# Attention with packed keys, then a token-mixing MLP, on one core: all steps in a new order, with TensorE's short steps spread over its blocks of 256 instructions

## The chip, the core and the metric

The kernel runs on one core of a Trainium2 chip. The core has a matrix engine (TensorE, in the profile PE, its weight loads PEld), a vector engine (VectorE, DVE), an activation engine (ScalarE, ACT), a general engine (GpSimd, POOL) and a queue engine (SyncE, SP). Each engine works through its own instructions in the order in which they were written, and waits on semaphores for what other engines or transfers must have done. The metric is the device time of the whole program in microseconds (us). The kernel before takes 109.34 us, the median of three runs.

## The reference

Eight batches, eight heads, 576 tokens, 64 wide; 32 packed queries p for each head. All inputs and the output are float32 in memory.

```python
def sm_attn(qq, kk, vv):
    s = scale * np.matmul(qq, kk.transpose(0, 1, 3, 2))
    s = s - np.max(s, axis=-1, keepdims=True)
    a = np.exp(s)
    a = a / (np.sum(a, axis=-1, keepdims=True) + 1e-09)
    return np.matmul(a, vv)
p_packed = sm_attn(p, k, v)
out = sm_attn(q, p_packed, p_packed)          # B, H, S, 64
...
x = out.transpose(0, 2, 1, 3).reshape(B, S, 512)
wq = x @ w_q                                  # 512 -> 64
wk = x @ w_k
W_tok = scale * np.einsum('bsd,btd->bst', wq, wk)
mixed = np.einsum('bst,btd->bsd', W_tok, x)
return np.maximum(mixed, 0.0) @ w_out
```

## The kernel before

The whole kernel is a list of some 700 steps, the string `ORDER`, and a loop at the end that walks through it. An item is `NAME.batch.part@ENGINE=banks`: `X1.2.0@A` is step X1 of batch 2, part 0, on ScalarE (A; V is VectorE, P is GpSimd), and `S1.2=4,5,2,3` is a TensorE step that writes the PSUM banks 4, 5, 2 and 3. No scheduler comes behind it: on each engine the instructions stand in the order of the items. Semaphores between engines are placed by the framework from what a step reads and writes, PSUM banks included: a step that writes a bank waits until the last reader of it is done.

For each batch b the steps are:

- Loads, all issued by GpSimd's queue: `LD.k`, `LD.v` (two transfers), `LD.q`; batch 0 has k in two halves `LD.g0` and `LD.h0` and q in two halves `LD.r0` and `LD.q0`, batch 7 `LD.r7` and `LD.q7`. `LD.P0` to `LD.P3` bring the packed queries, `LD.W0` and `LD.W1` w_k and w_q, `LD.O` w_out (tile `wout`). Each of k, v and q has four buffers (NL = 4). The loads turn float32 into bfloat16.
- `KT` (VectorE, line 244) turns k round in blocks of 32x32; `S1` (TensorE, lines 277 and 287) makes the scores of the packed queries; `X1` (ScalarE) their exponentials; `TE` (VectorE) turns them round. Batches 0 and 1 need no `TE`, but the block diagonal of p (`EC`, `EX`, `PB`); the others need `PX`.
- `PV` (TensorE, line 318) multiplies with v, whose buffers carry a block of ones for the sums (`SET.v`); `RC` and `PP` (VectorE) divide and mask, `PT` turns round. The result is p_packed.
- `QK` (TensorE, line 339) is p_packed times w_k and w_q, `QKE` copies it out of PSUM and `QD` (GpSimd) doubles a part of it.
- `QV` (VectorE) turns q round; `S2` (TensorE, line 376) makes the scores of the second attention, in parts 0, 1, 2 (batches 0, 1, 7) or 3 and 2; `X2` (ScalarE) their exponentials; `RS`, `RR` (VectorE) sums and reciprocals (for batch 5 `HA` on GpSimd halves the sum first); `AM` (VectorE or GpSimd, line 408) multiplies: the weights a.
- `AT` (TensorE, lines 417 and 422) turns a round, `AE` copies it out of PSUM; `WKQ` (TensorE, lines 444 and 449) makes wk and wq from it, `WE` copies; `GM` (line 470), `GE`, `Y` (line 480), `YE`, `MX` (line 495), `MR` (line 501) make the mixed tokens; `RL`, `RLR` and `RLF` (ScalarE or VectorE) the maximum with 0.
- `OT` (TensorE, line 543, four matmuls of 128x512 each; `OH` half as wide) multiplies with w_out; `OE`, `OEF` and `OEH` copy to SBUF; `ST`, `STF` and `STH` store, on SP's queue. SP first runs `HOLD.v7`, which waits for the last load of v, so that no store runs beside the loads before it.

`WARM.n=bank` (line 614) is n matmuls of 128x512 whose result nobody reads. They stand where TensorE would have nothing to do, the first 27 ahead of the first step S1.0. One block of TensorE's program in what follows is 256 instructions; each matmul is two, a weight load and the multiplication.

Eight PSUM banks are shared by all steps; `T["s1", b]`, `T["mx", b, i]` and the like hold which banks a later step reads. The step loop:

```python
else:
    bk = [int(z) for z in bk.split(",")] if bk else None
    steps[f[0]](*[int(z) for z in f[1:]], eng,
                bk[0] if bk and len(bk) == 1 else bk)
```

## Time and profile before

| | before |
|---|---|
| median of 3 runs | 109.34 us (109.15 to 109.53) |
| the profiled execution | 109.69 us |
| its span, first to last instruction | 107.6 us |
| granted TensorE clock | 1.0 throughout |
| busy: TensorE, VectorE, ScalarE, GpSimd | 96.4, 78.2, 66.3, 49.1 us |
| loads through GpSimd's queue | 15.08 MB |
| stores through SP's queue | 9.50 MB |

The profile is one execution. A line of the chain of waits has the start, the length and what ran or was waited for; `issue` is time in which the engine waited for nothing that the profile shows. A line of the timeline has start, length, engine, source line, operation, tiles and shapes, and in brackets the idle time before it with what ended that. A line of the groups has the count, then total busy time and the mean in ns of one, then idle time before them. The line of a helper (244 for all 32x32 transposes, 131 and 135 for copies) stands for all steps that use it. The loads keep the DMA engines busy from about 3 us to about 78 us, at some 210 GB/s.

### The profile page before, as it was taken

The numbers are of one execution on the slowest core, as the hardware profiler recorded it, in microseconds if no ns is written. First come the engines' busy times: TensorE is split into PE (matmuls) and PEld (weight loads), VectorE is DVE, ScalarE is ACT, GpSimd is POOL, SyncE is SP. The second block draws the span as 40 slices with busy tenths as digits, with TensorE's granted clock in tenths as the row PEclk, the third lists the DMA queues.
The fourth block names the chain that finished last, engine by engine and source line by source line (L and its number), as shares of the span: only waits on it lengthen the run. The fifth ranks groups of instructions, "written<-read, shape, count | busy, mean of one in ns | idle before, by whom it ended". The sixth has DMA issues, their size and how long they took to land.

```text
span 107.6 us, 3612 instructions
## 1 busy us (share of the span) xinstructions
PE 96.4 (90%) x1547; PEld 53.2 (49%) x1547; DVE 78.2 (73%) x151; ACT 66.3 (62%) x104; POOL 49.1 (46%) x75
## 2 busy tenths in 40 slices
...
GB/s 51 143 173 196 210 209 201 216 208 206 206 211 211 209 213 207 209 210 213 212 206 213 214 202 213 215 204 215 218 398 395 411 270 299 254 387 328 195 371 129
DMA packets 13935, 24.87 MB, mean 231 GB/s; under 512 B 2144, under 2 KB 7008, under 8 KB 13920
## 3 DMA queue, kind: packets, MB, share of 16 engines
q0 software_dynamic: 10016, 15.08, 78.7%
q1 hardware_dynamic: 3632, 9.50, 22.9%
q8 instruction: 12, 0.20, 0.7%
...
q14 instruction: 3, 0.02, 0.1%
...
## 4 chain that ended last, share of the span: by engine, by line
PE 60%; DMA 10%; POOL 7%; ACT 7%; DVE 6%; issue 5%; ACTq 0%; POOLq 0%; DVEq 0%
PE ps L543 26%; DMA wqk<-in_moe_w_q_dram 10%; PE ps L376 4%; PE ps L318 4%; PE ps L422 4%; PE ps L449 3%; PE ps L614 3%; PE ps L495 3%; PE ps L287 3%; PE ps L444 3%; DVE rs L397 2%; PE ps L470 2%; POOL a L408 2%; PE ps L339 2%; ACT aT L131 2%
## 5 line engine op out<-in xcount | busy, mean ns | idle before, releaser
L543 PE MATMUL ps<-wout,relu 128*128 128x512 bf16 x124 | 30.9, 380 | 0.5 <-ACT e1T L298 0.5
L408 POOL TENSOR_TENSOR a<-e,rr 128x256 bf16<-128x256 f32 (+2 forms) x15 | 15.9, 1070 | 23.3 <-ACT e L381 6.5
L614 PE MATMUL ps<-o 128*128 128x512 bf16 x79 | 21.1, 406 | 1.9 <-DVE o L138 1.9
L381 ACT ACTIVATE e<-ps 128x256 f32<-128x256 f32 (+2 forms) x19 | 11.2, 622 | 13.2 <-PE ps L376 13.0
L131 ACT ACTIVATE o<-ps 128x1024 f32<-128x1024 f32 (+2 forms) x18 | 15.8, 882 | 2.2 <-PE ps L543 2.1
L543 PEld LDWEIGHTS <-relu 128*128 128x128 bf16 x124 | 10.7, 98 | 11.7 <-issue 2.0
L244 DVE STREAM_TRANSPOSE kT<-k_sb 128x1152 uint32<-128x1152 uint32 (+1 forms) x9 | 11.2, 1243 | 3.2 <-DMA k_sb<-in_k_dram 3.2
L506 ACT ACTIVATE relu<-ps 128x1024 bf16<-128x1024 f32 (+1 forms) x11 | 13.0, 1218 | 0.6 <-PE ps L501 0.6
L397 DVE TENSOR_REDUCE rs<-e 128x16 f32<-128x512 f32 (+2 forms) x13 | 11.1, 856 | 2.4 <-ACT e L381 2.4
L614 PEld LDWEIGHTS <-o 128*128 128x128 bf16 x79 | 7.4, 104 | 10.4 <-issue 2.4
L244 DVE STREAM_TRANSPOSE qT<-q_sb 128x1152 uint32<-128x1152 uint32 (+1 forms) x10 | 11.0, 1107 | 0.0
L179 POOL DMA_DIRECT2D v_sb<-in_v_dram x16 | 10.2, 647 | 0.3 <-issue 0.3
L298 ACT ACTIVATE e1T<-ps 128x576 bf16<-128x576 f32 x12 | 7.3, 650 | 2.7 <-PE ps L287 2.6
L244 DVE STREAM_TRANSPOSE e<-e1T 128x576 bf16<-128x576 bf16 x12 | 8.7, 746 | 0.2
L295 ACT ACTIVATE e<-ps 128x1152 bf16<-128x1152 f32 x2 | 2.3, 1132 | 9.6 <-PE ps L277 9.6
L508 DVE TENSOR_SCALAR relu<-ps 128x1024 bf16<-128x1024 f32 (+1 forms) x7 | 7.7, 1131 | 0.1
L318 PE MATMUL ps<-v_sb,e 64*64 64x192 bf16 x288 | 7.7, 245 | 0.0
L376 PE MATMUL ps<-ppT,qT 64*128 64x64 bf16 x320 | 6.6, 190 | 1.3 <-issue 1.1
L376 PEld LDWEIGHTS <-qT 64*128 64x128 bf16 x320 | 5.7, 94 | 4.1 <-issue 2.1
L318 PEld LDWEIGHTS <-e 64*64 64x64 bf16 x288 | 5.8, 106 | 2.1 <-issue 1.4
L131 ACT ACTIVATE wkq<-ps 128x896 bf16<-128x896 f32 (+1 forms) x8 | 6.2, 778 | 1.0 <-PE ps L449 0.8
L449 PE MATMUL ps<-aT,pqk 128*128 128x256 bf16 (+1 forms) x48 | 6.7, 246 | 0.0
...
## 6 DMA issues: line engine op xcount, KB each, us to landing
out_dram<-o SPq DMA_DIRECT2D x14, 512.0 KB, 4.9
...
```

Of the source, the lines that this page charges most:

```text
L131: nc.scalar.activation(o, i, COPY)
L179: nc.gpsimd.dma_start(v_bufs[b % NL][halves(i), 0:7:2], src)
L244: nc.vector.transpose(o, i)
L318: nc.tensor.matmul(T["pv", b][halves(cc), i], lhsT, rhs, start=n == 0, stop=n == R - 1, skip_group_check=True)
L376: nc.tensor.matmul(ps[:, y, t - t0, i], lhsT, rhs, start=e == 0, stop=e == 1)
L381: nc.scalar.activation(e2[:, t0:t1].rearrange("a t (i y n) -> a y (t i) n", i=2, y=2), T["s2", b, c].rearrange("a y t i n -> a y (t i) n") ...
L397: nc.vector.tensor_reduce(rs[:, t0 * H:t1 * H], src, axis=AX, op=ADD)
L408: e.tensor_tensor(a2[:, t0:t1].rearrange("a t i (u l) -> a (t i u) l", l=L), e2v(b, c), T["rr", b][:, t0 * H:t1 * H].to_broadcast((P, (t1 ...
L449: nc.tensor.matmul(o, pqk[:, i, Dl:], aT[:, i, c0:c1], start=i == 0, stop=i == 1)
L506: nc.scalar.activation(o, i, RELU)
L543: nc.tensor.matmul(ps, lhsT, wout[:, j, :], start=j == 0, stop=j == NJ - 1)
L614: nc.tensor.matmul(ps, warm[:, 0:P], warm, start=True, stop=True)
```

## The change

Nothing but `ORDER` changes: the same steps in another sequence, some of them on another engine or in other banks.

```diff
--- before.py
+++ after.py
@@ -10,53 +10,53 @@
 TURN = tuple(range(8))
 
 ORDER = """
-LD.E1@A LD.E0@S LD.g0 LD.h0 SET.v2@P LD.r0 LD.W0 SET.pz0@V SET.aT1@V SET.aT0@V SET.warm@V SET.idf@V
-SET.v0@V SET.tab@A EC@V EX@V SET.aff@P LD.v0 KT.0.0@V PB.0.2@V SET.mask@V KT.0.1@V PB.0.3@V QV.0.0@V
-LD.q0 PB.0.1@A LD.k1 PB.0.0@P WARM.27=3 S1.0=0,1,2 X1.0.0@A WARM.12=3 PV.0.0=0,1 PV.0.1 RC.0@V LD.W1
-SET.v1@P LD.P0 LD.v1 PP.0.0@V PP.0.1@V QV.0.1@V PT.0@V SET.v3@P LD.q1 LD.P1 LD.P2 LD.P3 WARM.8=2
-S2.0.2=0,1 X2.0.2@A RS.0.2@V KT.1.2@V RR.0.2@V S2.0.1=4,5 S2.0.0=2,3 X2.0.1@A WARM.5=6 QK.0=0
-X2.0.0@A SET.idb@V RS.0.1@V RS.0.0@V QKE.0@V RR.0.1@V RR.0.0@V LD.k2 LD.O AM.0.1@P WARM.2=2
-S1.1=3,4,5 X1.1.0@A WARM.5=2 PV.1.0=4,5 PV.1.1 RC.1@V PP.1.0@V PP.1.1@V AM.0.0@V PT.1@V QV.1.2@V
-AT.0.1=3 WARM.5=0 AT.0.0=2 QK.1=4 QD.0@P LD.v2 AM.0.2@P LD.q2 WARM.4=5 S2.1.2=0,1 S2.1.0=6,7 PX@V
-X2.1.2@A AT.0.2=5 S2.1.1=0,1 X2.1.0@A AE.0.2@A X2.1.1@A RS.1.2@V AE.0.0@V RR.1.2@V WKQ.0.0=6,7 LD.k3
-AM.1.2@P WKQ.0.2 WARM.1=0 AT.1.2=1 AE.0.1@V RS.1.1@V QKE.1@A WKQ.0.1 RR.1.1@V AM.1.1@P LD.v3 LD.k4
-KT.2.2@V RS.1.0@V WE.0.0@A AE.1.2@A WE.0.1@A WARM.3=4 GM.0=6 GE.0@V RR.1.0@V AM.1.0@V S1.2=4,5,2,3
-AT.1.1=7 Y.0=0,1 X1.2.0@A AE.1.1@V X1.2.1@A LD.q3 QD.1@P YE.0@A WARM.3=6 AT.1.0=4 AE.1.0@A TE.2.1@V
-MX.0.1=0,1 MR.0=2,3 TE.2.0@V MX.0.0=4,5 RL.0.1@A RLR.0@A RL.0.0@A WKQ.1.0=6,7 WKQ.1.2 WKQ.1.1
-PV.2.0=0,1 PV.2.1 WE.1.0@V WE.1.1@V RC.2@V PP.2.1@V PP.2.0@V PT.2@V QV.2.2@V GM.1=6 GE.1@A WARM.1=7
-Y.1=4,5 OT.0.0=0,1 YE.1@A MR.1=4,5 MX.1.0=6,7 WARM.2=2 S2.2.3=2,3 RLR.1@A X2.2.3@A RL.1.0@V
-S2.2.2=4,5 OT.0.1 X2.2.2@A KT.3.2@V LD.v4 RS.2.4@V RR.2.4@V SET.aT2@V OE.0.0@A MX.1.1=6,7 OT.1.4=2
-S1.3=4,5,0,1 X1.3.0@A QK.2=3 OEF.1.4@A X1.3.1@A RL.1.1@A QKE.2@A TE.3.0@V AM.2.3@V TE.3.1@V
-OT.0.2=4,5 OT.0.3 LD.q4 LD.k5 AM.2.2@P LD.v5 QD.2@P AT.2.2=0 WARM.1=1 AT.2.3=6 PV.3.0=2,3 PV.3.1
-AE.2.3@A WKQ.2.0=6,7 OE.0.1@A KT.4.2@V AE.2.2@V RC.3@V WKQ.2.1 WKQ.2.2 WE.2.2@A S1.4=0,1,4,5
-PP.3.1@V PP.3.0@V PT.3@V QV.3.2@V OT.1.0=2,3 QK.3=6 GM.2=7 X1.4.1@A X1.4.0@A S2.3.2=4,5 QKE.3@A
-TE.4.1@V TE.4.0@V X2.3.2@A GE.2@A S2.3.3=0,1 X2.3.3@A Y.2=4,5 OT.1.1 YE.2@V RS.3.4@V MX.2.0=6,7
-MX.2.1=0,1 PV.4.0=4,5 PV.4.1 OE.1.0@A RR.3.4@V RC.4@V OT.1.2=2,3 PP.4.0@V PP.4.1@V LD.k6 LD.q5
-QD.3@P AM.3.3@P AM.3.2@P PT.4@V QV.4.2@V RL.2.1@A RL.2.0@A OT.1.3 MR.2=4,5 QK.4=0 RLR.2@V OE.1.1@A
-QKE.4@A AT.3.3=1 AE.3.3@V S2.4.3=6,7 S2.4.2=2,3 X2.4.2@A X2.4.3@A AT.3.2=5 WKQ.3.0=0,1 AE.3.2@V
-KT.5.2@V WKQ.3.1 WKQ.3.2 OT.2.2=2,3 WE.3.2@A RS.4.4@V S1.5=6,7,4,5 GM.3=1 OT.2.3 X1.5.0@A X1.5.1@A
-GE.3@V LD.v6 QD.4@P Y.3=6,7 OE.2.1@A OT.2.0=4,5 TE.5.0@V YE.3@V RR.4.4@V LD.q6 LD.k7 AM.4.3@P
-AM.4.2@P LD.v7 LD.r7 LD.q7 TE.5.1@V MX.3.0=6,7 MX.3.1=0,1 MR.3=2,3 RLR.3@A OT.2.1 PV.5.0=2,3
-RL.3.1@V KT.6.2@V RL.3.0@A OE.2.0@A PV.5.1 AT.4.3=6 AT.4.2=7 OT.3.0=0,1 AE.4.3@A RC.5@V PP.5.1@V
-PP.5.0@V AE.4.2@V QV.5.2@V PT.5@V S1.6=2,3,4,5 WKQ.4.0=6,7 X1.6.0@A X1.6.1@A WKQ.4.1 WKQ.4.2
-TE.6.0@V TE.6.1@V OT.3.1 WE.4.2@A S2.5.2=4,5 S2.5.3=2,3 X2.5.2@A OE.3.0@A GM.4=7 X2.5.3@A PV.6.0=4,5
-GE.4@V Y.4=6,7 PV.6.1 QK.5=0 YE.4@V RC.6@V MX.4.1=6,7 QKE.5@A MX.4.0=2,3 PP.6.0@V PP.6.1@V PT.6@V
-QV.6.2@V RL.4.1@A OT.3.2=0,1 HA.5@P RS.5.4@V RR.5.4@V AM.5.3@P OT.3.3 RL.4.0@A S2.6.2=6,7 S2.6.3=4,5
-X2.6.2@A MR.4=2,3 QK.6=7 X2.6.3@A OE.3.1@A RLR.4@V KT.7.2@V HOLD.v7 OT.3.4=6 OT.4.0=4,5 RS.6.4@V
-S1.7=0,1,2,3 QKE.6@A OEF.3.4@A X1.7.1@A X1.7.0@A QD.5@P AM.5.2@P QD.6@P AT.5.3=7 AE.5.3@V RR.6.4@V
-OT.4.1 AT.5.2=2 AE.5.2@A WKQ.5.0=0,1 AM.6.3@P AM.6.2@P WKQ.5.1 WKQ.5.2 OE.4.0@A OT.4.2=2,3 WE.5.2@A
-OT.4.3 GM.5=0 TE.7.1@V TE.7.0@V QV.7.0@V QV.7.1@V GE.5@V AT.6.3=7 AT.6.2=6 OE.4.1@A Y.5=0,1 AE.6.2@A
-YE.5@A AE.6.3@V PV.7.0=4,5 ST.0.0 ST.0.1 ST.1.4 ST.1.0 ST.1.1 ST.3.4 ST.2.0 ST.3.1 ST.4.0 PV.7.1
-MR.5=0,1 RC.7@V RLR.5@A MX.5.1=6,7 MX.5.0=2,3 RL.5.1@A PP.7.0@V PP.7.1@V WKQ.6.0=0,1 WKQ.6.1 WKQ.6.2
-PT.7@V RL.5.0@V OT.5.4=4 WE.6.2@A S2.7.0=2,3 S2.7.2=0,1 S2.7.1=6,7 X2.7.2@A RS.7.2@V GM.6=5 X2.7.0@A
-OEF.5.4@A X2.7.1@A OT.5.2=0,1 GE.6@V RS.7.0@V RR.7.2@V AM.7.2@P Y.6=2,3 QK.7=5 YE.6@V RR.7.0@V
-OT.5.3 AT.7.2=2 QKE.7@A RS.7.1@V RR.7.1@V AE.7.2@A AM.7.1@V AM.7.0@P QD.7@P MX.6.1=6,7 MX.6.0=4,5
-RL.6.0@V RL.6.1@V OE.5.1@A OT.5.0=2,3 AT.7.0=0 AT.7.1=1 AE.7.0@A OT.5.1 AE.7.1@A WKQ.7.0=4,5 WKQ.7.2
-WKQ.7.1 WE.7.0@V OT.6.0=6,7 OE.5.0@V WE.7.1@A GM.7=4 OT.6.1 GE.7@A ST.5.4 ST.3.0 ST.5.1 ST.4.1
-ST.2.1 ST.5.0 OE.6.0@A ST.6.0 Y.7=2,3 MR.6=4,5 YE.7@V RLR.6@V OT.6.2=0,1 MX.7.1=6,7 MR.7=4,5
-MX.7.0=2,3 RLR.7@V OT.6.3 RLF.7.0.1@V RLF.7.0.0@V RLF.7.1.0@A RLF.7.1.1@A OT.7.4=5 OE.6.1@A OH.7.0=2
-OT.7.2=6 ST.6.1 OEF.7.4@A OEH.7.0@A OEF.7.2@A STH.7.0 ST.7.4 STF.7.2 OT.7.1=2 OEF.7.1@A STF.7.1
-OT.7.0=5 OH.7.1=6 OEF.7.0@A OEH.7.1@A STF.7.0 STH.7.1
+LD.E0@S LD.E1@A SET.pz0@V SET.aT0@V SET.warm@V SET.tab@A EC@A EX@V SET.v1@V SET.idf@V PB.0.2@V LD.h0
+SET.v3@P LD.g0 SET.v0@P LD.v0 LD.q0 SET.mask@P PB.0.0@P PB.0.3@V KT.0.1@V KT.0.0@V PB.0.1@V
+WARM.21=1 S1.0=0,2,4 X1.0.0@A WARM.5=3 PV.0.0=0,1 PV.0.1 RC.0@V QV.0.1@V PP.0.0@V PP.0.1@V LD.r0
+LD.k1 LD.W1 LD.W0 SET.aff@P SET.idb@V PT.0@V QV.0.0@V WARM.11=2 S2.0.2=0,1 S2.0.0=2,3 LD.v1 LD.P3
+LD.q1 LD.P2 SET.v2@V KT.1.2@V LD.P1 LD.P0 S2.0.1=4,5 X2.0.1@A X2.0.0@A X2.0.2@A RS.0.1@V SET.aT1@V
+RS.0.0@V RR.0.1@V RS.0.2@V RR.0.2@V RR.0.0@V AM.0.0@V AM.0.2@V SET.aT2@V WARM.10=6 S1.1=0,1,2
+X1.1.0@A WARM.6=3 PV.1.0=0,1 PV.1.1 AT.0.0=3 AT.0.2=5 LD.k2 LD.v2 LD.q2 AM.0.1@V RC.1@V PP.1.0@V
+AE.0.2@V PP.1.1@V PT.1@V AT.0.1=2 WARM.3=4 QK.1=0 QKE.1@A QK.0=1 QKE.0@A AE.0.0@V LD.k3 QD.0@P
+QD.1@P LD.O QV.1.2@V WARM.6=3 S2.1.2=0,1 S2.1.1=4,5 S2.1.0=6,7 AE.0.1@A X2.1.1@A PX@V WARM.2=2
+WKQ.0.0=4,5 WKQ.0.2 RS.1.1@V X2.1.0@A WKQ.0.1 X2.1.2@A WE.0.0@A RS.1.0@V RR.1.1@V WE.0.1@A KT.2.2@V
+RS.1.2@V RR.1.0@V RR.1.2@V AM.1.0@V LD.v3 AM.1.1@P LD.k4 AM.1.2@V WARM.3=1 GM.0=0 WARM.3=5 AT.1.1=4
+S1.2=2,3,6,7 GE.0@A AE.1.1@A Y.0=0,1 YE.0@A AT.1.0=4 AE.1.0@V X1.2.1@A AT.1.2=0 X1.2.0@A AE.1.2@A
+WARM.1=1 MR.0=6,7 WKQ.1.0=4,5 MX.0.1=2,3 RLR.0@V TE.2.0@V TE.2.1@V WKQ.1.2 WKQ.1.1 MX.0.0=6,7
+WARM.1=0 PV.2.0=0,1 QV.2.2@V WE.1.0@A PV.2.1 WE.1.1@A RC.2@V PP.2.1@V GM.1=4 GE.1@V PP.2.0@V
+RL.0.0@A RL.0.1@A PT.2@V WARM.6=5 S2.2.2=2,3 KT.3.2@V S2.2.3=0,1 QK.2=4 Y.1=6,7 X2.2.2@A X2.2.3@A
+QKE.2@A YE.1@V RS.2.4@V WARM.3=2 MX.1.1=6,7 S1.3=0,1,2,3 X1.3.1@A X1.3.0@A RL.1.1@A OT.0.0=4,5
+OT.0.2=2,3 OT.0.3 TE.3.1@V RR.2.4@V AM.2.2@V OT.0.1 AT.2.2=0 OE.0.1@A TE.3.0@V PV.3.0=6,7 PV.3.1
+LD.q3 LD.v4 LD.q4 QD.2@P LD.k5 AM.2.3@V LD.k6 OE.0.0@A AE.2.2@A AT.2.3=2 MR.1=0,1 MX.1.0=4,5 RC.3@V
+AE.2.3@V PP.3.0@V KT.4.2@V PP.3.1@V PT.3@V RLR.1@A RL.1.0@A WARM.1=3 WKQ.2.0=0,1 WKQ.2.2 WKQ.2.1
+OT.1.4=2 WE.2.2@A LD.v5 S1.4=6,7,4,5 OEF.1.4@A GM.2=0 X1.4.1@A QV.3.2@V OT.1.0=2,3 GE.2@A X1.4.0@A
+Y.2=4,5 YE.2@A S2.3.2=6,7 S2.3.3=0,1 X2.3.2@A TE.4.0@V TE.4.1@V X2.3.3@A MX.2.1=4,5 OT.1.1
+MX.2.0=0,1 PV.4.0=6,7 PV.4.1 RS.3.4@V RL.2.1@A OE.1.0@A RL.2.0@A OT.1.2=4,5 RC.4@V RR.3.4@V PP.4.1@V
+PP.4.0@V LD.q5 AM.3.3@P OT.1.3 PT.4@V QV.4.2@V OE.1.1@A QK.4=7 MR.2=0,1 QK.3=6 AM.3.2@V AT.3.3=2
+AT.3.2=3 S2.4.2=4,5 AE.3.3@V RLR.2@A QKE.3@A AE.3.2@A QKE.4@A X2.4.2@A S2.4.3=0,1 KT.5.2@V X2.4.3@A
+QD.3@P WKQ.3.0=2,3 WKQ.3.2 WKQ.3.1 OT.2.2=4,5 WE.3.2@A RS.4.4@V S1.5=0,1,6,7 GM.3=2 X1.5.1@A OT.2.3
+KT.6.2@V GE.3@A X1.5.0@A Y.3=6,7 OT.2.0=2,3 YE.3@A OE.2.1@A MX.3.0=6,7 MX.3.1=0,1 RR.4.4@V TE.5.1@V
+TE.5.0@V RL.3.0@A OT.2.1 RL.3.1@V PV.5.0=4,5 OE.2.0@A LD.v6 LD.q6 AM.4.3@P LD.k7 LD.v7 QD.4@P
+AM.4.2@V PV.5.1 S1.6=0,1,6,7 RC.5@V AT.4.3=2 AT.4.2=3 PP.5.0@V PP.5.1@V OT.3.0=4,5 X1.6.0@A X1.6.1@A
+AE.4.3@V AE.4.2@V PT.5@V TE.6.0@V QV.5.2@V TE.6.1@V WKQ.4.0=6,7 WKQ.4.1 WKQ.4.2 OT.3.1 QK.5=2
+WE.4.2@A OE.3.0@A GM.4=3 GE.4@V MR.3=6,7 S2.5.3=0,1 Y.4=4,5 RLR.3@V YE.4@V QKE.5@A X2.5.3@A
+PV.6.0=2,3 LD.r7 LD.q7 QD.5@P PV.6.1 S2.5.2=4,5 RC.6@V MX.4.1=0,1 PP.6.1@V PP.6.0@V X2.5.2@A
+MX.4.0=6,7 OT.3.2=4,5 RL.4.1@A HA.5@P OT.3.3 RL.4.0@A PT.6@V QV.6.2@V RS.5.4@V S2.6.2=0,1 X2.6.2@A
+S2.6.3=2,3 MR.4=6,7 RR.5.4@V QK.6=0 X2.6.3@A RLR.4@V OT.3.4=1 AM.5.3@P AM.5.2@P KT.7.2@V OE.3.1@A
+OT.4.0=2,3 RS.6.4@V S1.7=4,5,6,7 OEF.3.4@A QKE.6@A AT.5.3=1 AT.5.2=0 OT.4.1 AE.5.3@V HOLD.v7
+X1.7.1@A X1.7.0@A AE.5.2@V RR.6.4@V OE.4.0@A WKQ.5.0=4,5 QD.6@P AM.6.3@P AM.6.2@P WKQ.5.2 WKQ.5.1
+OT.4.2=0,1 TE.7.1@V QV.7.0@V TE.7.0@V WE.5.2@A OT.4.3 OE.4.1@A ST.0.0 ST.0.1 ST.1.4 GM.5=2 GE.5@V
+QV.7.1@V AT.6.3=4 AT.6.2=5 Y.5=2,3 PV.7.0=6,7 YE.5@A AE.6.2@A AE.6.3@V PV.7.1 MR.5=0,1 MX.5.1=2,3
+RC.7@V RLR.5@A MX.5.0=4,5 RL.5.1@A PP.7.1@V PP.7.0@V WKQ.6.0=0,1 WKQ.6.2 WKQ.6.1 PT.7@V RL.5.0@V
+OT.5.4=6 WE.6.2@A S2.7.2=4,5 S2.7.0=2,3 S2.7.1=0,1 OEF.5.4@V X2.7.2@A X2.7.0@A GM.6=7 RS.7.2@V
+OT.5.2=4,5 RR.7.2@V RS.7.0@V GE.6@A X2.7.1@A AM.7.2@P RR.7.0@V Y.6=2,3 QK.7=7 RS.7.1@V AT.7.2=0
+RR.7.1@V AE.7.2@V QKE.7@V YE.6@A OT.5.3 AM.7.0@P OE.5.1@A MX.6.1=0,1 MX.6.0=2,3 RL.6.1@V RL.6.0@V
+OT.5.0=6,7 AM.7.1@P QD.7@P AT.7.0=5 AT.7.1=4 AE.7.0@A OT.5.1 AE.7.1@A WKQ.7.0=0,1 WKQ.7.2 WKQ.7.1
+WE.7.0@V OT.6.0=2,3 WE.7.1@A OE.5.0@V GM.7=0 OT.6.1 GE.7@A ST.1.0 ST.1.1 ST.3.4 ST.2.0 ST.3.0 ST.3.1
+ST.4.0 ST.5.4 ST.4.1 OE.6.0@A ST.5.1 ST.2.1 ST.5.0 ST.6.0 MR.6=4,5 Y.7=6,7 OT.6.2=0,1 RLR.6@V YE.7@V
+MX.7.1=4,5 MR.7=2,3 MX.7.0=6,7 RLF.7.1.1@A RLF.7.1.0@A RLR.7@V OT.6.3 OT.7.4=2 RLF.7.0.0@V
+RLF.7.0.1@V OE.6.1@A ST.6.1 OH.7.0=6 OT.7.2=0 OEF.7.4@A OEH.7.0@A OEF.7.2@A STH.7.0 ST.7.4 STF.7.2
+OT.7.1=6 OT.7.0=2 OEF.7.1@A OH.7.1=7 STF.7.1 OEF.7.0@A OEH.7.1@A STF.7.0 STH.7.1
 """
 
 
```

On TensorE the number of matmuls goes from 1547 to 1550: 82 fillers in place of 79, 21 of them (before: 27) ahead of S1.0. All other TensorE steps are the same; in front of S1.4, of S1.5, of S1.7 and behind PV.7 they are also the same set. In TensorE's program the ends of the blocks of 256 fall on other steps. From GpSimd to VectorE go AM.0.1, AM.0.2, AM.1.2, AM.2.2, AM.3.2, AM.4.2, SET.v1 and SET.v2; from VectorE to GpSimd AM.7.1, SET.mask and SET.v0. From VectorE to ScalarE go EC, QKE.0, AE.0.1, GE.0, AE.1.1, WE.1.0, WE.1.1, RL.1.0, AE.2.2, YE.2, RLR.2, AE.3.2, GE.3, YE.3, GE.6 and YE.6; from ScalarE to VectorE PB.0.1, AE.0.2, AE.1.0, RLR.0, GE.1, YE.1, AE.2.3, RLR.3, AE.4.3, AE.5.2, OEF.5.4, QKE.7 and AE.7.2. The loads stand in this order: h0 g0 v0 q0 r0 k1 W1 W0 v1 P3 q1 P2 P1 P0 k2 v2 q2 k3 O v3 k4 q3 v4 q4 k5 k6 v5 q5 v6 q6 k7 v7 r7 q7.

## The prediction

> **What bounds it now.** I read the shares first, then the chain of work that ended last, then busy time by stretches, then the timeline of the first 24 us.
>
> ```profile
> span 107.6 us, 3612 instructions
> ...
> PE 96.4 (90%) x1547; PEld 53.2 (49%) x1547; DVE 78.2 (73%) x151; ACT 66.3 (62%) x104; POOL 49.1 (46%) x75
> ...
> q8 instruction: 12, 0.20, 0.7%
> ```
>
> TensorE is busy for 90% of the span, and queue q8 brings 12 packets of together 0.20 MB, 16 KB each: TensorE's program of 3094 instructions (two for each of 1547 matmuls), in pieces of 256. The chain:
>
> ```profile
> 50.42 1.12 issue
> 51.54 0.28 PE ps L376 x6
> ...
> 63.80 0.97 PE ps L543 x4
> 64.77 0.87 PE ps L318 x36
> 65.63 0.55 PE ps L422 x8
> 66.24 0.86 PE ps L543 x4
> ...
> 71.16 0.35 issue
> 71.51 0.24 PE ps L480 x2
> ```
>
> Twice TensorE stands still while nothing that the profile shows holds it: 1.12 us inside S2.3.3 (line 376) and 0.35 us inside Y.4 (line 480). Busy time by stretches (columns: stretch and its length, then busy time and number of instructions of TensorE, weight loads, VectorE, ScalarE, GpSimd, then granted clock, DMA share, GB/s):
>
> ```profile
> 9.54:48.02 38.48, 35.69 (x651) 20.24 (x650) 29.54 (x59) 20.14 (x34) 21.08 (x33) 1.00 1.16 209
> 18.24:47.80 29.56, 26.87 (x510) 15.49 (x513) 26.88 (x52) 17.43 (x30) 17.32 (x27) 1.00 1.15 209
> 46.65:72.21 25.56, 23.65 (x514) 14.13 (x514) 21.32 (x38) 21.16 (x30) 11.41 (x16) 1.00 1.14 210
> 48.02:103.00 54.98, 53.05 (x885) 29.97 (x870) 43.36 (x74) 43.78 (x67) 19.87 (x25) 1.00 0.99 264
> 51.54:71.51 19.97, 19.24 (x384) 11.02 (x383) 17.13 (x29) 17.03 (x22) 10.18 (x13) 1.00 1.14 210
> ```
>
> From one resumption to the other TensorE starts 384 matmuls, that is 768 instructions, three times 256. So both stalls sit at the same place of a 256-block. The packets of q8 fit that: one lies in the stretch 49.0 to 50.1, one in 69.0 to 70.1, none in the 8 us ahead of the first, and the packet that belongs to the next block after the first stall lies in 55.1 to 56.3.
>
> ```profile
> q8 instruction: 1, 0.02, 5.3%
> q8 instruction: 1, 0.02, 5.8%
> q8 instruction: 1, 0.02, 5.5%
> ```
>
> 5.3% of 16 engines in 1.1 us is 0.93 us for a packet, and TensorE goes on 1.4 us after either stretch has ended. Counting 128 matmuls back from the stalls, the blocks began inside PV.3 at about 45.8 and with OT.3.0 at about 66.1. A block's successor was thus usable 5.7 and 5.4 us after the block began; TensorE's own work in them was 1.12 and 0.35 us shorter, 4.6 and 5.1 us. The third packet would give 56.3 + 1.4 - 51.5 = 6.2 us, but that block is longer, and no stall shows.
>
> Otherwise the kernel has two parts. Up to the start of S1.4 (47.60) TensorE idles 38.48 - 35.69 = 2.79 us and runs 52 fillers (WARM) after S1.0. From 48.02 on it idles 54.98 - 53.05 = 1.93 us only: 1.47 at the two block ends, and this:
>
> ```profile
> L422 PE MATMUL ps<-idb,a 128*128 128x128 bf16 x16 | 1.2, 220 | 0.4 <-POOL a L408 0.4
> ```
>
> AT.3.3 waits 0.4 us for AM.3.3 on GpSimd.
>
> **The change, first part.** In front of S1.4 both orders hold the same TensorE steps, apart from fillers: 61 instead of 52 after S1.0 (82 instead of 79 in all). Behind it there are none. So S1.4 is the cut.
>
> ```profile
> 6.18 0.79 DVE L244 STREAM_TRANSPOSE kT<-k_sb 128x576 uint32<-128x576 uint32 x1 [2.34 <-DMA k_sb<-in_k_dram]
> 8.87 0.22 DVE L135 COPY o<-o 32x256 bf16<-32x256 bf16 x1
> 9.54 1.23 PE L277 MATMUL ps<-o,kT 128*64 128x128 bf16 x36
> 10.71 2.76 PE L614 MATMUL ps<-o 128*128 128x512 bf16 x12
> 10.82 1.13 ACT L295 ACTIVATE e<-ps 128x1152 bf16<-128x1152 f32 x1 [6.53 <-PE ps L277]
> 13.40 0.94 PE L318 MATMUL ps<-v_sb,e 64*64 64x192 bf16 x36
> ...
> 18.24 1.38 DVE L244 STREAM_TRANSPOSE kT<-k_sb 128x1152 uint32<-128x1152 uint32 x1 [0.84 <-DMA k_sb<-in_k_dram]
> ...
> 19.70 0.78 POOL L174 DMA_DIRECT2D wout<-in_moe_w_out_dram  x1
> ...
> 23.22 0.17 DVE L322 RECIPROCAL rec<-ps 128x2 f32<-128x2 f32 x1 [1.64 <-PE ps L318]
> ...
> 47.60 0.49 PE L287 MATMUL ps<-kT,pT 32*32 32x288 bf16 x32
> ```
>
> S1.0: the second half of k0 can be there 288 KB at 209 GB/s = 1.4 us after the first (6.18), at 7.6; mask setting no longer stands on VectorE ahead of its transpose; 7.6 + 0.79 + 0.22 (PB.0.1 is now last) gives 8.65 against 9.54. The 21 first fillers are over by then (27 took until 9.54, and the last run at 2.69 / 12 = 0.22 us each). X1.0.0 ends 8.65 + 1.28 + 1.13 = 11.06. v0 moves directly behind k0, in front of r0 and W0: 7.6 + 2 x 1.4 = 10.4. So PV.0 starts at 11.1, where the 12 fillers held it until 13.40. That lead of 2.3 us goes no further than KT.1.2, which waits for k1 (18.24), and k1 has only the 64 KB of W0 less ahead of it: 0.3 us at 209 GB/s (bounds: 0, and 1.1 us if the order of the packets mattered too). From there VectorE's queue is the clock of this part: 26.88 us busy of the 29.56 from KT.1.2 to the end of PT.3.
>
> ```profile
> L508 DVE TENSOR_SCALAR relu<-ps 128x1024 bf16<-128x1024 f32 x5 | 6.4, 1299 | 0.1
> L408 DVE TENSOR_TENSOR a<-e,rr 128x512 bf16<-128x512 f32 x3 | 2.4, 794 | 0.1
> L489 DVE TENSOR_SCALAR y<-ps 128x256 bf16<-128x256 f32 x5 | 2.1, 417 | 3.2 <-PE ps L480 3.2
> L135 DVE COPY aT<-ps 128x1024 bf16<-128x1024 bf16 x3 | 2.1, 691 | 0.4 <-PE ps L422 0.3
> L135 DVE CAST wkq<-ps 128x448 bf16<-128x448 f32 x3 | 1.8, 613 | 0.4 <-PE ps L444 0.4
> L244 DVE STREAM_TRANSPOSE ppT<-pp 128x128 uint32<-128x128 uint32 x8 | 2.4, 300 | 0.2
> L408 POOL TENSOR_TENSOR a<-e,rr 128x256 bf16<-128x256 f32 x8 | 5.2, 656 | 10.5 <-ACT e L381 6.5 <-ACT e1T L298 2.5 <-DVE rr L402 1.5
> ```
>
> Into this stretch come AM.0.1 (0.79), AM.0.2, AM.1.2 and AM.2.2 (128x256, never run on VectorE here: half of 0.79 = 0.40 from below, GpSimd's 0.66 from above; 0.45 taken, since VectorE's row of the same operation is the nearer), AE.2.3 (0.69), and seven small ones (RS.0.2, AE.0.2, AE.1.0, RLR.0, GE.1, YE.1, SET.aT1), none over YE's 0.42, taken at 0.34, 2.4 together: 5.2. Out go RL.1.0 (1.30), WE.1.0 and WE.1.1 (2 x 0.61), and six small ones (SET.idb, QKE.0, AE.0.1, GE.0, AE.1.1, AE.2.2) at 0.34, 2.0 together: 4.5. Net +0.7 (with AM at 0.40 and 0.66: +0.5 and +1.3). Of its 2.68 us idle, RC.1's wait of 1.64 goes, because the softmax steps of S2.0 now stand ahead of RC.1; but RS.1.1 must wait some 0.65 for X2.1.1 (VectorE is through PX sooner than TensorE through six fillers and S2.1), and RC.3 and AE.2.3 some 0.9 for PV.3 and AT.2.3, which stand behind four OT. These are estimates; their sum leaves -0.1. PT.3 then ends at 47.80 - 0.3 + 0.7 - 0.1 = 48.1. S1.4 needs banks 6 and 7 from PP.3.1, which ends as PT.3 (0.30) begins: 47.8 against 47.60. So the first part costs +0.2, with bounds of -1.1 (k1 at its bound, and 0.5 less of the new waits) and +1.2 (AM at 0.66, k1 no sooner, 0.1 for wout below). TensorE alone would have been there sooner (47.60 - 0.85 + 9 x 0.22 - 2.79 = 45.9), so the nine fillers stand in its waits; without that cover they cost up to 2.0.
>
> LD.O moves on GpSimd's queue from behind k2 to behind k3, QD.0 and QD.1. v2, q2 and k3 gain 512 KB, 2.4 us; wout loses three loads of 576 KB, 8.3 us.
>
> ```profile
> wout<-in_moe_w_out_dram POOLq DMA_DIRECT2D x1, 512.0 KB, 11.3
> ```
>
> Issued at 19.70 it landed at 31.0; now at 39.3. Its first reader OT.0.0 stands behind S1.3 and QK.2, near 39.6. This is covered by 0.3 us only; a later landing moves OT.0.0, which the wait for AE.2.3 behind it (0.3) partly absorbs. On SP only ST.3.0, ST.4.1 and ST.5.1 change places among the stores behind HOLD.v7; they run beside TensorE's work, and the last eight stores are as before.
>
> **Second part.** 53.05 us of TensorE work stay. The block from PV.3 gains OT.1.4 (0.97), AT.2.3 (0.55), MR.1, MX.1.0, Y.2 and a filler (some 0.9) and gives up 12 matmuls of PV.3 (0.3) and QK.3 (0.4): 4.6 + 1.7 = 6.3 us, over the 5.7 that it needs. The block from S1.6 gains AT.4.3, AT.4.2 (0.6), QK.5 and MR.3 (0.5) and gives up S2.5.2 and most of PV.6 (0.7): 5.1 + 0.4 = 5.5 against 5.4. I leave 0.2 of the 1.47 us. AT.3.3's wait for AM.3.3 shrinks, since QK.3 (0.4) now stands between S2.3.3, where that chain begins, and AT.3.3, and only Y.2 (0.2) has left: of 0.4 us I leave 0.2 (bounds 0 and 0.4). New waits come from banks. S1.6 now uses 0 and 1, which RL.3.1 (1.30, VectorE) frees: it begins when TE.5.0 lets PV.5 (0.87) begin, so up to 0.45. OT.3.0 needs PP.5.1, behind RL.3.1, AM.4.2, RC.5 and PP.5.0 (some 2.6 us), while TensorE has PV.5, S1.6 and AT.4 (1.9) to do: up to 0.7 less S1.6's wait. S2.7.2 now stands first of S2.7 and needs RL.5.0. TensorE reaches each somewhat after that earliest moment; I take 0.4 for the three (bounds 0 and 1.2) and 0.2 for others. Idle: 0.2 + 0.2 + 0.4 + 0.2 = 1.0 in place of 1.93, so -0.9.
>
> **The sum.** The last matmul, the eviction behind it and the last store keep their order, so the end moves with TensorE: +0.2 - 0.9 = -0.7. The profiled execution took 109.69 (107.6 of span and 2.1 around it), so 109.0; the median of 109.34 is 0.35 below that execution, which gives 108.6.
>
> **Rivals.** Larger gain: part of PV.0's lead gets past k1, and the first part ends at its lower bound, 1.3 us below what I took: 107.3. For it speaks that v2, q2 and k3 come 2.4 us sooner; against it, that VectorE has little room left in which to use it.
>
> The fetch is still late: if a block needs the 6.2 us of the third packet, the new blocks of 6.3 and 5.5 us still lose 0 and 0.7, and with 0.1 for their neighbours 0.8 comes back in place of 0.2: 109.2. Against it: where it cost something, 5.4 to 5.7 were measured.
>
> It is not the fetch: then both stalls belong to something else and stay (1.47), the new waits of 0.6 come on top, 0.2 of AT.3.3's goes, and the first part costs its 0.2: 109.34 + 0.2 + 0.6 - 0.2 = 109.9. The page Runtime: NRT & Kernel Launch of the Trainium skill, section Instruction fetch mechanics, says that a 16 KiB block of 256 instructions is fetched while the one before it runs, and that crossing a boundary is mostly hidden; by that rule this would be the outcome. Against it here: the 384 matmuls between the stalls, and the packets that end 1.4 us ahead of each resumption.
>
> VectorE sets the pace (the slower side). In the first part its queue comes out at the upper bound, +1.2. In the second part its busy time hardly grows (AM.3.2, AM.4.2, AE.4.3 and RLR.3 come, 1.9; YE.2, RLR.2, AE.3.2, GE.3 and YE.3 go, 1.7), but KT.6.2 now stands ahead of TE.5 and RL.3.1, and the three bank waits reach their bound of 1.2: 0.2 + 0.2 + 1.2 + 0.2 - 1.93 = -0.1. Together +1.1, 110.4. It decides from the point where S1.4's lateness and the three waits add up to more than the 1.5 us of the stalls. For it: VectorE is 91% busy up to PT.3 and 83% (21.32 of 25.56) from RC.3 to RC.6; against it: TensorE idles only 1.93 us in the second part, with much the same work on VectorE.
>
> **Chances.** Forecast 0.47 (its own range 107.9 to 109.1), larger gain 0.12, fetch still late 0.11, not the fetch 0.06, VectorE 0.24. What this kernel's measurement can tell from no change is 0.3%, 0.33 us: faster is under 109.01. Faster: 0.44 + 0.12 + 0.02 = 0.58; same: 0.03 + 0.08 + 0.02 = 0.13; slower: 0.01 + 0.04 + 0.24 = 0.29. The range goes from 107.2, at the larger gain, to 110.5, where VectorE's case ends.
>
> **What would show it.** Right: no "issue" piece over 0.3 us on TensorE in the chain between S1.4 and S2.7; S1.0 at 8.5 to 8.9, PV.0 near 11.1, KT.1.2 still started by k1 at 17 to 18.3, S1.4 at 47 to 48.5, TensorE idle behind it near 1 us. Wrong in the first part: S1.4 after 49, then fillers or wout (a wait of OT.0.0 on the DMA). Wrong in the second: "issue" again 128 matmuls apart from a block start, or TensorE waiting for VectorE at S1.6, OT.3.0 and S2.7.2 for over 1.2 us together.

## The result, and the profile after

The changed kernel takes 108.74 us, the median of 19 runs, against 109.44 us for the kernel before (19 runs): ratio 0.9893, 95% interval 0.9857 to 0.9929. The forecast was a gain of 0.7 us, to 108.6. (Ratios leave disturbed executions out, here and below, so that they can differ from those of the medians.) The gain is as forecast, its two parts are not:

| | before | forecast | after |
|---|---|---|---|
| S1.0 begins | 9.54 | 8.65 | 9.18 |
| PV.0 begins | 13.40 | 11.1 | 13.85 |
| S1.4 begins (the cut) | 47.60 | 47.8 | 49.01 |
| from there to the end of the last matmul | 55.41 | 54.5 | 53.37 |
| TensorE idle in that second part | 1.93 | 1.0 | 0.43 |
| profiled execution | 109.69 | 109.0 | 108.79 |

The first part came out 1.4 us later than before, not 0.2, and the second 2.0 us shorter, not 0.9. The second part by stretches (columns as in the prediction), first the kernel before, then the changed one:

```profile
47.60:103.01 55.41, 53.48 (x905) 30.18 (x902) 43.78 (x75) 44.11 (x67) 20.29 (x25) 1.00 1.00 264
```

```profile
9.18:49.01 39.83, 37.63 (x627) 21.01 (x627) 29.63 (x62) 21.42 (x35) 18.73 (x31) 0.96 1.16 209
11.53:14.95 3.42, 3.32 (x33) 1.65 (x36) 0.00 (x0) 0.05 (x1) 1.54 (x3) 0.50 1.11 210
49.01:102.38 53.37, 52.94 (x903) 29.68 (x902) 43.88 (x75) 43.76 (x69) 19.39 (x23) 1.00 1.01 268
```

Both "issue" stalls of TensorE are gone. Of the idle 53.37 - 52.94 = 0.43 us the largest piece is 0.14, at AT.3.3. The middle row of the second fence is new: for 3.42 us TensorE was granted half its clock. The page shows it in its 40 slices (the mean of both rates in the slices at either edge), and TensorE's timeline shows what stood ahead of it:

```profile
PEclk9999679999999999999999999999999999999999
```

```profile
6.70 1.24 PE L614 MATMUL ps<-o 128*128 128x512 bf16 x5
9.18 1.23 PE L277 MATMUL ps<-o,kT 128*64 128x128 bf16 x36 [1.24 <-DVE o L135]
11.63 2.29 PE L614 MATMUL ps<-o 128*128 128x512 bf16 x5 [1.23 <-ACT e L295]
13.85 1.44 PE L318 MATMUL ps<-v_sb,e 64*64 64x192 bf16 x36
15.23 1.04 PE L614 MATMUL ps<-o 128*128 128x512 bf16 x4
```

The 21 fillers were over at 7.94, S1.0 waited for PB.0.1 until 9.18 (1.24 us), and the five fillers behind S1.0 waited 1.23 us for X1.0.0 on ScalarE, although they write bank 3 and X1.0.0 reads banks 0, 2 and 4: its source is one access pattern that steps over every second bank, and bank 3 lies inside the range that this spans. Then the five fillers took 2.29 us, at half rate, and PV.0, which could have begun when X1.0.0 was done (11.6), began at 13.85. ScalarE and VectorE show the rest:

```profile
10.45 1.13 ACT L295 ACTIVATE e<-ps 128x1152 bf16<-128x1152 f32 x1 [7.07 <-PE ps L277]
```

```profile
8.10 0.78 DVE L244 STREAM_TRANSPOSE kT<-k_sb 128x576 uint32<-128x576 uint32 x1 [1.14 <-DMA k_sb<-in_k_dram]
18.47 1.34 DVE L244 STREAM_TRANSPOSE kT<-k_sb 128x1152 uint32<-128x1152 uint32 x1
```

KT.1.2 began at 18.47 without any wait: k1 had landed at 16.63, and it was the work ahead of it on VectorE, behind PV.0, that was late. So two theories were to be tried. Theory one: the gain of the second part is the fetch of TensorE's program (rival: those stalls belong to their steps, or the second part was shorter only because its inputs had been ready longer). Theory two: the loss of the first part is idle time around S1.0 and the clock that fell after it (rival: VectorE's queue and the added fillers).

### The profile page after: what moved, and what is told of

Same layout as the page of the kernel before. It is cut to its first block, busy times and chain, and to the rows that moved or that the text cites. A ratio compares the mean times of both kernels' runs of the same rounds, so it can differ in the third digit from the quotient of the medians.

```text
span 106.9 us, 3614 instructions
## 1 busy us (share of the span) xinstructions
PE 96.7 (90%) x1550; PEld 53.0 (50%) x1550; DVE 77.6 (73%) x149; ACT 67.6 (63%) x107; POOL 45.7 (43%) x74
## 4 chain that ended last, share of the span: by engine, by line
PE 55%; DMA 21%; DVE 9%; ACT 5%; POOL 3%; issue 3%; ACTq 0%; DVEq 0%; POOLq 0%
PE ps L543 25%; DMA k_sb<-in_k_dram 21%; PE ps L376 4%; PE ps L614 4%; PE ps L318 3%; PE ps L495 3%; PE ps L422 3%; PE ps L449 3%; PE ps L444 2%; PE ps L470 2%; DVE aT L135 2%; DVE kT L244 2%; POOL a L408 2%; PE ps L339 2%; ACT e L381 2%
## 5 line engine op out<-in xcount | busy, mean ns | idle before, releaser
L614 PE MATMUL ps<-o 128*128 128x512 bf16 x82 | 22.7, 415 | 3.1 <-DVE o L138 1.8
L408 POOL TENSOR_TENSOR a<-e,rr 128x1024 bf16<-128x1024 f32 (+2 forms) x10 | 12.5, 1263 | 19.0 <-DVE rr L402 12.5
L506 ACT ACTIVATE relu<-ps 128x1024 bf16<-128x1024 f32 (+1 forms) x12 | 14.3, 1228 | 0.6 <-PE ps L501 0.6
L244 DVE STREAM_TRANSPOSE kT<-k_sb 128x1152 uint32<-128x1152 uint32 (+1 forms) x9 | 11.1, 1232 | 2.4 <-DMA k_sb<-in_k_dram 2.4
L244 DVE STREAM_TRANSPOSE qT<-q_sb 128x1152 uint32<-128x1152 uint32 (+1 forms) x10 | 11.1, 1107 | 0.0
L131 ACT ACTIVATE wkq<-ps 128x448 bf16<-128x448 f32 (+1 forms) x10 | 7.1, 732 | 2.5 <-PE ps L449 1.9
L318 PEld LDWEIGHTS <-e 64*64 64x64 bf16 x288 | 6.3, 113 | 2.2 <-issue 1.5
L322 DVE RECIPROCAL rec<-ps 128x2 f32<-128x2 f32 x8 | 1.3, 164 | 8.4 <-PE ps L318 8.3
```

The source lines that it names most:

```text
L131: nc.scalar.activation(o, i, COPY)
L244: nc.vector.transpose(o, i)
L318: nc.tensor.matmul(T["pv", b][halves(cc), i], lhsT, rhs, start=n == 0, stop=n == R - 1, skip_group_check=True)
L408: e.tensor_tensor(a2[:, t0:t1].rearrange("a t i (u l) -> a (t i u) l", l=L), e2v(b, c), T["rr", b][:, t0 * H:t1 * H].to_broadcast((P, (t1 ...
L506: nc.scalar.activation(o, i, RELU)
L614: nc.tensor.matmul(ps, warm[:, 0:P], warm, start=True, stop=True)
```

## The experiments

| kernel | median us | ratio to before, 95% | S1.0 | S1.4 | S1.4 to last matmul |
|---|---|---|---|---|---|
| before | 109.4 to 109.7 | | 9.54 | 47.60 | 55.41 |
| b_block | 109.42 | 0.9956 (0.992 to 0.9992) | 9.66 | 48.18 | 55.03 |
| b_240 | 108.54 | 0.9912 (0.9872 to 0.9951) | 9.59 | 47.32 | 54.69 |
| b_96 | 108.01 | 0.9845 (0.9803 to 0.9887) | 10.52 | 48.25 | 53.94 |
| b_phase | 107.82 | 0.9856 (0.9819 to 0.9893) | 8.94 | 46.63 | 53.85 |
| h_ba | 109.27 | 0.9975 (0.9947 to 1.0004) | 10.53 | 48.27 | 54.26 |
| after | 108.74 | 0.9893 (0.9857 to 0.9929) | 9.18 | 49.01 | 53.37 |
| a_phase | 107.85 | 0.9861 (0.9824 to 0.9899) | 9.81 | 47.85 | 53.79 |
| a_bank | 108.08 | 0.9878 (0.983 to 0.9927) | 9.78 | 47.63 | 53.55 |
| a_fill | 107.81 | 0.9817 (0.9782 to 0.9852) | 9.78 | 48.05 | 53.35 |
| a_both | 107.50 | 0.98 (0.9762 to 0.9838) | 9.42 | 47.75 | 53.33 |
| a_w | 107.17 | 0.9794 (0.9745 to 0.9842) | 10.07 | 47.20 | 53.35 |
| a_gw | 107.89 | 0.9848 (0.9805 to 0.9892) | 9.35 | 47.12 | 53.93 |
| a_best | 107.84 | 0.9758 (0.9674 to 0.9841) | 9.97 | 47.09 | 53.40 |

The last three columns are of one profiled execution each, the medians of 6 to 12 runs (after: 19; before: 11 to 17 in each of four series). The item lists of b_phase, h_ba, a_bank and a_phase are up to two lines shorter, so that line 541 or 542 in their rows is the 543 of the others.

**Is it the fetch?** In four kernels no step of the kernel before is moved; only fillers change their shape, so that the program's blocks of 256 end at other steps.

```diff
 b_phase:
-WARM.27=3
+WARM.4=3 WARM.71.128=3
 b_96:
-WARM.27=3
+WARM.10=3 WARM.65.128=3
 b_block:
-WARM.27=3 ... WARM.12=3 ... WARM.8=2 ... WARM.5=6
+WARM.4=3 WARM.87.128=3 ... WARM.46.128=3 ... WARM.30.128=2 ... WARM.2=6 WARM.11.128=6
 b_240: as b_block, but WARM.5=6 is kept
```

(`WARM.71.128` is 71 fillers of 128 columns.) b_phase:

> The kernel before, with 23 of the 27 fillers ahead of S1.0 made into 71 of 128 columns: 96 instructions more in about the same time, no step moved. Fetch theory: the blocks end elsewhere, the shortest are then 5.35 and 5.46 us long, and the stalls of 1.12 us in S2.3.3 and 0.35 us in Y.4 go, but for up to 0.3 us; the time falls by 1.0 to 1.5 us against the kernel before, to 107.9 to 108.4 (ratio 0.986 to 0.991). Rival (stalls of S2.3.3 and Y.4 themselves, or of a wait that is not seen): both are still there, time within 0.3 us of the kernel before.

b_96:

> The kernel before, with 17 of the 27 first fillers made into 65 of 128 columns: 96 instructions more as in b_phase, but this time with the time on TensorE kept (3.62 and 3.63 us; in b_phase the fillers were 0.9 us shorter and S1.0 began 0.6 us sooner). Fetch theory: no issue stall over 0.3 us behind S1.4, 53.6 to 54.1 us from S1.4 to the last matmul in place of 55.4, time 107.8 to 108.4. Rival (b_phase gained by its shorter fillers, or by luck of its loads): 108.9 or more.

b_block:

> The kernel before, with 46 fillers of 512 columns ahead of QK.0 made into 174 of 128 columns. In the runs so far one of 512 took 0.213 us and one of 128 0.056 us, so the time is the same (9.8 and 9.7 us), but TensorE's program has 128 matmuls, 256 instructions, more: one whole block, so that from there on the blocks end at the same steps as before. Fetch theory: the stalls of about 1.1 us in S2.3.3 and 0.35 us in Y.4 are there as in the kernel before, and the time is within 0.4 us of it, 109.0 to 109.8. Rival (narrow fillers as such made the kernel with 96 instructions more faster): no stalls, 107.5 to 108.3.

b_240:

> The kernel before, with 43 fillers ahead of QK.0 made into 163 others of which all but none are narrower: 23 of the first 27 into 87, the 12 into 46 and the 8 into 30 of 128 columns, 240 instructions more in the same time (9.2 and 9.1 us). The blocks then end 240 instructions sooner in the list, that is 16 later than in the kernel before. Fetch theory: the two short blocks become 4.7 and 4.2 us long without stalls, against 4.65 and 4.84 before, so the stall near Y.4 grows from 0.35 us to 0.9 to 1.3 and the one in or near S2.3.3 stays at 0.7 to 1.1; time 0.4 to 1.0 us above b_block, 109.7 to 110.5. Rival (stall lengths have nothing to do with the lengths of the blocks): as b_block or b_96.

Where 96 more instructions move the block ends, both stalls are gone but for a piece of under 0.3 us, and where one more whole block brings the ends back, they are back, at the same steps. TensorE's timeline of b_block, then of b_240:

```profile
50.31 0.69 PE L376 MATMUL ps<-ppT,qT 64*128 64x64 bf16 x34
51.71 0.27 PE L376 MATMUL ps<-ppT,qT 64*128 64x64 bf16 x6 [0.70 <-issue]
...
71.06 0.24 PE L480 MATMUL ps<-pp,g 64*64 64x128 bf16 x2
71.70 0.24 PE L480 MATMUL ps<-pp,g 64*64 64x128 bf16 x2 [0.39 <-issue]
```

```profile
50.46 0.24 PE L480 MATMUL ps<-pp,g 64*64 64x128 bf16 x2 [0.22 <-ACT g L131]
51.20 0.24 PE L480 MATMUL ps<-pp,g 64*64 64x128 bf16 x2 [0.49 <-issue]
...
69.99 0.33 PE L318 MATMUL ps<-v_sb,e 64*64 64x192 bf16 x6
70.66 0.44 PE L318 MATMUL ps<-v_sb,e 64*64 64x192 bf16 x10 [0.33 <-issue]
```

In b_block TensorE stops inside S2.3.3 and between two matmuls of Y.4, as before. In b_240 the block ends lie 8 matmuls later, and so do the stops: S2.3.3 runs through, and Y.2 and PV.6 are broken instead. With the issue stalls taken off, the second part of the old order is of nearly one length: 55.41 - 1.47 = 53.94 (before), 55.03 - 0.70 - 0.39 = 53.94 (b_block), 54.69 - 0.49 - 0.33 = 53.87 (b_240), 53.94 - 0.29 = 53.65 (b_96, whose one piece of 0.29 stands ahead of MR.4). The expectations for b_96 and b_block held, but that the first stall of b_block is 0.70 and not 1.1. b_phase came out 0.1 below its range, its fillers being 0.9 us shorter. For b_240 the place was right and the size was not: 0.82 us of stalls in place of 1.6 or more, and a time of 108.54, below the expected 109.7 to 110.5, and below b_block where it was to be above. Its second short block lost only 0.33 us because its successor was fetched sooner, as the packets of queue q8 and the matmuls' starts in the trace show (times in us, worked out from the records):

```
          block begins  packet starts  packet ends  TensorE goes on
before        45.72         49.09         50.03        51.54
before        66.08         69.09         70.05        71.51
b_block       46.30         49.46         50.40        51.71
b_block       66.25         69.27         70.23        71.70
b_240         45.60         48.88         49.85        51.20
b_240         66.13         68.14         69.03        70.66
a_phase       34.38         37.88         38.83        40.14
a_gw          63.69         67.34         68.31        69.69
```

From the end of the packet it is always 1.3 to 1.6 us; from the block's begin to the packet it is 2.0 to 3.7 us. So there is no fixed length that a block needs: 4.5 us in one case, 6.0 in another.

a_phase puts the same 96 instructions into the new order (on top of a_bank, below):

```diff
-WARM.21=1
+WARM.1=1 WARM.68.128=1
```

> As a_bank, and of the 21 fillers ahead of S1.0 20 of 512 columns become 68 of 128 columns: about the same time on TensorE, but 48 matmuls, 96 instructions, more, so that every later block of 256 ends 96 instructions sooner in the list of steps. Nothing else moves. Fetch theory: the blocks that now begin in PV.2.0 and in S2.5.3 are 4.7 and 4.75 us long, under the 5.4 to 5.7 that the next block needs, so TensorE stands still with nothing to wait for, 0.7 to 1.0 us inside S1.3 and 0.7 to 0.9 us inside S2.6.3, where it does not now; the time is 0.9 to 1.9 us above a_bank. Rival (the stalls of the kernel before belonged to their steps or to a wait that is not seen): no such stall, time within 0.3 us of a_bank.

```profile
38.94 0.48 PE L286 MATMUL ps<-kT,pT 32*32 32x288 bf16 x32
40.14 0.61 PE L542 MATMUL ps<-wout,relu 128*128 128x512 bf16 x2 [0.72 <-issue]
...
73.05 0.78 PE L375 MATMUL ps<-ppT,qT 64*128 64x64 bf16 x40
74.17 0.23 PE L500 MATMUL ps<-wkq,y 64*128 64x64 bf16 x4 [0.34 <-ACT e L380]
```

The first stall is there as expected: 0.72 us behind S1.3, in a place where a_bank stands 0.23 us for wout. In the second short block there is a pause of 0.34 us only, and a wait for ScalarE ends last in it. So a_phase lost 0.5 us against a_bank from S1.3 to OT.0.0 and 0.24 behind S1.4, and its profiled execution is 0.4 us longer (108.01 and 107.62); the 0.9 to 1.9 us expected did not come, and by their medians the two cannot be told apart: the stall came where the theory had it, the time is the rival's.

**Is the second part shorter in its own right?** The hybrid takes everything up to S1.4 from the kernel before and the rest from the new order:

```diff
 before, up to its S1.4 (from S1.2 on banks 0,1 and 6,7 exchanged)
+the steps of the changed kernel that are then left, in its order
```

> A hybrid: the kernel before up to S1.4, and all steps that are then left in the changed order. From S1.2 on the first part has banks 0 and 1 exchanged with 6 and 7, so that the two parts fit together. The blocks of 256 end within 6 instructions of where they end in the changed kernel. Theory (the first part of the new order costs 1.4 us, the second gains 2.0): S1.4 starts at 47.4 to 47.8, no issue stall over 0.3 us, 53.4 to 53.8 us from S1.4 to the last matmul, time 107.2 to 107.9 (ratio 0.980 to 0.986). As predicted on record (first part +0.2, second -0.9) it would be 108.4 to 108.7. Rival (the second part was shorter only because its inputs had been ready longer, the first part being late): S1.4 at 47.6 and 54.4 us or more behind it, with waits at S1.6, OT.3.0 and S2.7.2, time 108.4 or more.

The time missed the theory's range and lies where the rival had it (108.4 or more); the waits that the rival named, at S1.6, OT.3.0 and S2.7.2, did not come: none is over 0.07 us. By the profile three things add up. S1.0 began at 10.53, 1 us later than in the profile of before (see the last section; whether it did in the other eleven runs is not known). Behind S1.4 the seam costs: GM.2 waits for WE.2.2, which in the old first part stands later:

```profile
48.27 0.50 PE L285 MATMUL ps<-kT,pT 32*32 32x288 bf16 x32
49.34 0.45 PE L468 MATMUL ps<-wkq,a 128*128 128x64 bf16 x10 [0.58 <-ACT wkq L129]
...
51.82 0.21 PE L374 MATMUL ps<-ppT,qT 64*128 64x64 bf16 x2 [0.31 <-issue]
```

And the row at 51.82 is a fetch stall of 0.31 us: the short block begins at PV.3, so part of it lies in the old first part, which the expectation had left out. But from S1.5 to the end of the last matmul the hybrid takes 102.53 - 60.52 = 42.01 us, the changed kernel 102.38 - 60.36 = 42.02, the kernel before 103.01 - 60.30 = 42.71, 0.35 of it the stall in Y.4. All three begin S1.5 within 0.22 us of each other, so a late first part is not what makes this stretch shorter; for the stretch ahead of it the hybrid decides nothing. The table does: in a_bank, a_both and a_w (below) S1.4 begins at 47.20 to 47.75, about where it does in the kernel before, and the second part still takes 53.33 to 53.55 us.

**What made the first part late?** a_bank is to take away the idle time behind S1.0, a_fill the one ahead of it, a_both both:

```diff
 a_bank:
-WARM.5=3
+WARM.5=5
 a_fill:
-WARM.21=1
+WARM.25=1
 a_both: both
```

a_bank:

> The changed kernel with one bank number changed: the five fillers behind S1.0 write bank 5 in place of bank 3, so that they need not wait for X1.0.0, which reads banks 0, 2 and 4. Theory (false bank wait, then a lower clock): the 1.22 us of idle time behind S1.0 go, only the 1.24 us ahead of it are left, the granted clock stays at 1.0 from 5 us on, PV.0 starts at 11.7 in place of 13.85 (9.18 + 1.28 of S1.0 + 1.13 of X1.0.0), S1.4 at 47.8 to 48.2 in place of 49.01, and the time falls by 0.8 to 1.3 us against the changed kernel, to 107.4 to 107.9 (ratio to the kernel before 0.981 to 0.986). Rival (VectorE's queue and the added fillers made the first part longer, not the wait or the clock): PV.0 comes sooner, S1.4 stays at 48.7 or later, and the time changes by under 0.3 us. Second rival (the gap ahead of S1.0 alone lowers the clock): a stretch of about 3.4 us at 0.5 is still there, PV.0 at about 12.5.

a_fill:

> The changed kernel with 25 in place of 21 fillers ahead of S1.0, bank 3 kept: the idle time ahead of S1.0 is filled, the wait of the five fillers for X1.0.0 stays. Theory (the two idle times together lower the clock): granted clock 1.0 from about 5 to 7 us on, PV.0 starts 3.5 us after S1.0 (1.28 + 1.17 of wait + 5 x 0.213) in place of 4.67, time 107.9 to 108.4. Rival (the wait behind S1.0 alone lowers the clock): about 3.4 us at 0.5 behind S1.0, PV.0 4.6 us after S1.0, time 108.6 or more.

a_both:

> The changed kernel with 25 fillers ahead of S1.0 and the five behind it in bank 5: neither idle time. Theory: the clock stays at 1.0 in all executions, PV.0 2.4 to 2.6 us after S1.0, median 107.2 to 107.8, highest under 108.3 (a_bank, which keeps the idle time ahead of S1.0, went from 107.14 to 108.74). Rival (a_bank's spread comes from the loads, not from the clock): median 107.8 to 108.3 with the same spread.

TensorE's timeline of a_fill, then of a_both:

```profile
9.78 1.23 PE L277 MATMUL ps<-o,kT 128*64 128x128 bf16 x36 [0.53 <-DVE o L135]
12.24 1.24 PE L614 MATMUL ps<-o 128*128 128x512 bf16 x4 [1.23 <-ACT e L295]
13.41 0.94 PE L318 MATMUL ps<-v_sb,e 64*64 64x192 bf16 x36
```

```profile
9.42 1.24 PE L277 MATMUL ps<-o,kT 128*64 128x128 bf16 x36
10.82 1.03 PE L614 MATMUL ps<-o 128*128 128x512 bf16 x4 [0.16 <-issue]
11.88 0.94 PE L318 MATMUL ps<-v_sb,e 64*64 64x192 bf16 x36
```

In all three the clock stays up, and the fillers run at full rate. (In a_bank's profiled execution the idle time ahead of S1.0 was 0.69 us and not 1.24, the fillers having run longer; but a_phase, which has the same bank 5, stood still there for 2.52 us and kept its clock too.) PV.0 follows S1.0 by 2.46 us in a_both and a_bank (12.24 - 9.78), by 3.63 in a_fill, which keeps the wait for X1.0.0, and by 4.67 in the changed kernel: 1.2 us of that is the wait, 1.0 the clock. S1.4 comes at 47.63, 48.05 and 47.75, where 47.8 had been forecast, in place of 49.01; the rival, VectorE's queue and the fillers, would have kept it there. a_both's median lies in its range, its highest run (108.44) just over it; a_fill's median is 0.1 us under its range. a_bank missed it (108.08 against 107.4 to 107.9): two of its six runs took 108.7, one of them with a mean granted clock of 0.984, which is what 3.4 us at half rate make in 107. So filling the idle time ahead of S1.0 looks like the surer cure, though the intervals of a_bank and a_fill overlap. In the 19 runs of the changed kernel the same can be seen: eight have 0.984 and took 108.69 to 109.48; of the other eleven seven took 107.4 to 108.0 and four 108.7 to 108.8, which this does not explain.

**Does a lead get past k1?** a_w moves the loads of w_k and w_q behind v1 (on top of a_both); a_gw also moves the memset SET.v3 from between the halves of k0:

```diff
 a_w:
-LD.k1 LD.W1 LD.W0 ... LD.v1 LD.P3
+LD.k1 ... LD.v1 LD.W1 LD.W0 LD.P3
 a_gw, as a_w and:
-LD.h0 SET.v3@P LD.g0 SET.v0@P LD.v0 ... WARM.25=1
+LD.h0 LD.g0 SET.v0@P LD.v0 SET.v3@P ... WARM.23=1
```

> As a_both, with the loads W1 and W0 (64 KB each) behind v1 in place of between k1 and v1. Theory (as in the prediction: after PV.0 the first part waits for k1, at KT.1.2): k1 lands 0.4 to 1.0 us sooner than the 17.8 of a_both, KT.1.2 begins as it lands, S1.1 follows 1.4 us later, at 18.2 to 18.8; wout, which lands at 39.4 whatever stands ahead of it, holds OT.0.0, so that S1.4 is at most 0.5 us sooner; time 107.0 to 107.5. Rival (the queue's order between k1 and W does not matter to when k1 lands): no difference from a_both.

> As a_w, with the memset SET.v3 behind the load of v0 in place of between the two halves of k0, and 23 fillers ahead of S1.0. Theory: the second half of k0 is issued 0.5 us sooner and lands at 7.4 to 7.6, S1.0 begins at 8.5 to 8.9 (the prediction's 8.65) and PV.0 2.45 us later, but KT.1.2 still begins as k1 lands, so S1.1 and all behind it are within 0.3 us of a_w and so is the time. Rival (the lead gets past k1): S1.4 and the time 0.5 us or more sooner than a_w.

KT.1.2 in a_both, a_w and a_gw, in this order:

```profile
17.78 1.38 DVE L244 STREAM_TRANSPOSE kT<-k_sb 128x1152 uint32<-128x1152 uint32 x1 [1.71 <-DMA k_sb<-in_k_dram]
```

```profile
17.53 1.38 DVE L244 STREAM_TRANSPOSE kT<-k_sb 128x1152 uint32<-128x1152 uint32 x1 [0.80 <-DMA k_sb<-in_k_dram]
```

```profile
17.66 1.38 DVE L244 STREAM_TRANSPOSE kT<-k_sb 128x1152 uint32<-128x1152 uint32 x1 [1.66 <-DMA k_sb<-in_k_dram]
```

In all three it is k1's landing that starts it. a_gw has S1.0 0.72 us ahead of a_w (though at 9.35, not 8.5 to 8.9: the second half of k0 landed at 8.0, 1.45 us behind the first), and S1.4 0.08 us: the lead is lost there, as forecast. k1 started KT.1.2 only 0.25 us sooner in a_w than in a_both, less than expected (S1.1 at 19.14, not 18.2 to 18.8), and the medians (107.17 and 107.50) cannot be told apart. a_gw's profiled execution was 0.74 us longer than a_w's, not within 0.3; 0.40 of it is a fetch stall in PV.6.0:

```profile
68.79 0.50 PE L318 MATMUL ps<-v_sb,e 64*64 64x192 bf16 x14
69.69 0.68 PE L318 MATMUL ps<-v_sb,e 64*64 64x192 bf16 x22 [0.40 <-issue]
```

That is the block from S1.6 on, which the prediction had put at 5.5 us against the 5.4 needed; here 6.0 us passed from its begin to the matmul behind the stall. a_best, on top of a_w, moves the block ends away from it:

```diff
-WARM.25=1 ... WARM.11=2
+WARM.4=1 WARM.80.128=1 ... WARM.40.128=2
```

> As a_w, with 21 of the 25 first fillers and the 11 ahead of S2.0.2 made into 120 of 128 columns: the same time (6.8 and 6.7 us), 88 matmuls or 176 instructions more. In a_w's own times the shortest block in which loads still run is then 5.7 us long, against 5.3 without (S1.6 to PV.6.0, the block at whose end a_gw stood still for 0.40 us). Fetch theory: no issue stall over 0.15 us between S1.4 and S1.7 in the profiled execution, and a time 0 to 0.4 us below a_w, 106.8 to 107.2. Rival (that block's stalls are rare, or the gain lies within what the measurement can tell): no difference from a_w, 107.0 to 107.5.

Its profile has no such stall, PV.6 running through in one piece, but its runs lie between 106.28 and 108.29 us, its median over the expected range, and its interval overlaps a_w's nearly whole: inconclusive. a_fill, a_both and a_w beat both kernels, with intervals that end below where the changed kernel's begins; which of them is the fastest is not settled.

## Why the prediction was right, and where it was not

The sum was right, 0.7 us, by luck: two terms were mis-sized by about the same amount in opposite directions. Nor is the median a time that the changed kernel settles at: seven of its 19 runs took 107.4 to 108.0 us, twelve 108.69 to 109.48, and the median lies at the lower edge of the larger group.

*First part, forecast +0.2, measured +1.4 (beyond its bound of +1.2).* The +0.2 itself holds once the idle time around S1.0 is gone: S1.4 then comes at 47.63 to 48.05 (47.8 had been forecast); its single estimates on VectorE were not measured one by one. What failed is the step "So PV.0 starts at 11.1". S1.0 was 0.5 us late (the second half of k0 landed at 8.07, not 7.6: 1.92 us behind the first and not 1.4, because the memset SET.v3 stands between their two issues on GpSimd; without it, in a_gw, it was 1.45), and PV.0 another 2.2: I had costed X1.0.0 but not looked at which banks its read covers, so the wait of the fillers was missed, and I had taken the clock as given, because the profile of before had 1.0 throughout. "KT.1.2 still started by k1" failed with it, and holds in a_both, a_w and a_gw. No run leaves the nine added fillers out, but a_both, with four more of them, has S1.4 at 47.75, so they cost little or nothing, as forecast. wout landed at 39.25 by the trace (forecast 39.3; three loads of 576 KB, at 1024 bytes to the KB, are 8.5 us at 209 GB/s and not 8.3, so that this is closer than the working was), with OT.0.0 at 41.23; in a_bank, whose first part is sooner, OT.0.0 waited 0.23 us for it, as the forecast's thin cover of 0.3 had it.

*Second part, forecast -0.9, measured -2.0.* The mechanism was right. The fetch: of 1.47 us 0.2 were to stay; none did in this execution, though a_gw shows that the block from S1.6 can still lose 0.40. The fixed need of 5.4 to 5.7 us from one block's begin to the next, on which the forecast rested, did not hold: it was 4.5 to 6.0 us. AT.3.3's wait: 0.14 left, where 0.2 was taken. The waits for banks at S1.6, OT.3.0 and S2.7.2 (0.4) were too high: at the first two there is no gap, at S2.7.2 one of 0.08, and in a_both, whose first part is 1.3 us sooner, there is again none at the first two and 0.07 at S2.7.2. On top came 53.48 - 52.94 = 0.54 us of TensorE's busy time, with the same steps. The ends of matmuls are modelled, so waits too short to show as gaps may sit in there; where this time went stays open. Without its stalls the old second part takes 53.65 to 53.94 us, so that about 1.5 of the 2.0 us are the fetch.

*Rivals.* "It is not the fetch" falls by b_96 and b_block. The Trainium skill's page Runtime: NRT & Kernel Launch, section Instruction fetch mechanics, calls a block's crossing mostly hidden; most blocks here agree, but the two stalls of 1.12 and 0.35 us do not. "The fetch is still late" and "VectorE sets the pace" did not come; the second had the wrong cause for a late first part. "Larger gain" has the number that the changed kernel's best runs (107.4) and a_both reach, but not their mechanism: the lead does not get past k1.

And a gain of this size needs no new order: with 17 fillers cut into 65 the kernel before is at 0.9845 (0.9803 to 0.9887), no slower than the changed one at 0.9893 (0.9857 to 0.9929).
